# Score steps of two batches moved to stand with the transposes of the step before, and four unused transposes put ahead of a sweep's matmuls

## The chip, the cores and the metric

The kernel runs on one core of one Trainium2 chip, in one launch. The metric is the device time in microseconds (us). Lower is better. The engines' names are those of the profile: PE is TensorE (matmuls and transposes), PEld its weight loads, DVE VectorE, ACT ScalarE, POOL GpSimd, SP the queue that issues the DMAs.

## The reference

Attention over 4 batches, 12 heads, 448 rows and 64 columns a head, with q and k normalised by their root mean square, is followed by a gated layer (768 to 1536 to 768) and a layer with a squared ReLU (768 to 2048 to 768), all in fp32:

```python
q_n, k_n = rmsnorm(q, g_q), rmsnorm(k, g_k)
scores = q_n @ k_n.T / sqrt(64)                 # per batch and head, 448 x 448
attn = exp(scores - max); attn /= attn.sum() + 1e-9
x = (attn @ v)                                  # back to 1792 tokens x 768
x = (sigmoid(x @ w_gate) * (x @ w_val)) @ w_out
h = x @ w_in2
out = (maximum(h, 0) ** 2) @ w_out2             # 1792 x 768
```

## The kernel before

The work is done in four sweeps (`sweep(s)`, L506 to L603), one for each batch of 448 tokens. A sweep takes the attention output of its batch through both layers in 68 blocks of weights: 24 blocks for gate and val, 12 for the first output layer, 16 for the second layer's input, 16 for its output. An fp32 product is split into a high and a low part and made of three matmuls (`mm3`, L495 to L499), each 128 x 128 weights by 448 columns. This text calls those the wide matmuls: L497, L498, L499, 18 a block, 936 in a sweep. The last 16 blocks use matmuls of 384 columns (L596, L597, L598).

While sweep s runs, the attention of batch s+1 is made beside it. `slots_of` (L619 to L760) writes that attention as a list of slots, and the loop at the end (L867 to L884) runs one or two slots after each block. `later(n, ...)` puts a follow-up n blocks on, `mid` puts one into the next block. Batches 2 and 3 (made beside sweeps 1 and 2) use the branch `b > 1`. A pair of heads has e = 0 and 1; each head has its 448 rows in two halves c2 = 0 and 1. The steps of a half, and their letters here:

- S, the score step (`do_s2`): four matmuls of 448 columns with 112 columns of weights (L392) into a PSUM tile `att`; then the maximum on DVE (L399, L402), two exponentials on ACT (L411) and the scaling on DVE (L419 to L422).
- T, the transposes (`do_c2`): eight transposes of that half's exponentials, in two groups of four with 128, 128, 128 and 64 output rows (L431), then copies on ACT (L441, L442) and remainders on DVE (L447, L449).
- V, the product with v (`do_pv2`): seven matmuls of 448 columns (L457, L459), then L463 on ACT and L469 on DVE. After the second head of a pair `x_hi` (L329, ACT) and `x_lo` (L333, DVE) write the pair's rows of the next sweep's input.
- A (`do_a2`): eight transposes of q and k of the next pair (L241), then `a_hi` (L368, L369 on ACT), `a_lo` (L376, L379 on DVE) and `a_dma` (L386), which copies halves of `qs` between partitions.

The pool `att` has two tiles, and S, T, V and A all take one. `qs` has one buffer: the next pair's can be written when the last S of the pair has read the present one. In the slots before, S, T, S, A, V and T of a head stand one after the other, mostly one to a slot. Instructions on one engine run in the order in which the scheduler put them, which takes from the program's order what its own timing holds ready.

Of the kernel before, what the change touches and what calls it, by code (L numbers as in the profile page):

```python
# [17 lines left out]
def attention_moe_moe2_kernel(  # L18
# [14 lines left out]
    nc = tc.nc  # L33
    B, H, S, D = q.shape
# [8 lines left out]
    QR = S // QC  # L43
    NF = S // 128
    TAIL = S - 128 * NF
# [17 lines left out]
    ident = const.tile([128, 128], F32, name="ident")  # L63
# [9 lines left out]
    def att_tile():  # L73
        return att_p.tile([128, 2, 512], F32, tag="att", name="att")
# [281 lines left out]
    def split_v(st):  # L356
        t = st.pop("v")
        vs = one.tile([128, NF + 1, 4, D], F32R, tag="vs", name="vs")
        nc.scalar.copy(out=vs[:, :, 0::3], in_=t)
        nc.vector.tensor_tensor(out=vs[:, :, 1:3], in0=t, in1=vs[:, :, 0::3].bitcast(F32), op=ALU.subtract)  # L360
        st["vs"] = vs
# [26 lines left out]
    def s_mm2(st, e, c2, ps):  # L388
        for i in range(2):
            c = 2 * c2 + i  # L390
            for z in range(2):
                nc.tensor.matmul(  # L392
                    out=ps[:QR, i, :S], lhsT=st["qs"][:, e, z, c * QR:(c + 1) * QR], rhs=st["ks"][:, e],
                    start=(z == 0), stop=(z == 1))
        st["s", e, c2] = ps

    def s_max2(st, e, c2):
        nm = sm_p.tile([QR, 2], F32, tag="nm", name="nm")
        nc.vector.tensor_reduce(out=nm, in_=st["s", e, c2][:QR, :, :S], axis=AX.X, op=ALU.max, negate=True)  # L399
        rq = st["ms"][:, 1].rearrange("p (c h) -> p c h", h=2)[:, 2 * c2:2 * c2 + 2, e]  # L400
        with tc.high_priority(offset=200):
            nc.vector.tensor_tensor(out=nm, in0=nm, in1=rq, op=ALU.mult)  # L402
        st["nm", e, c2] = nm
# [21 lines left out]
    def c_mm2(st, e, c2):  # L425
        ps = att_tile().rearrange("p a (k c) -> p (a k) c", k=2)
        p = st.pop(("p", e, c2))
        for i in range(2):
            for kc in range(NF + 1):
                n = 128 if kc < NF else TAIL  # L430
                nc.tensor.transpose(  # L431
                    ps[:n, kc, i * QR:(i + 1) * QR], p[:, i, kc * 128:kc * 128 + n], ident[:QR, :QR])
        if c2 == 0:
            parts = one.tile([128, NS, S], F32R, tag="pt", name="parts")
            st["ph", e], st["pl", e] = parts[:, 0:NF + 1], parts[:, NF + 1:NS]
        st["c", e, c2] = ps

    def c_hi(st, e, c2):
        ps, ph = st["c", e, c2], st["ph", e]
        cs = slice(c2 * QW, (c2 + 1) * QW)  # L440
        nc.scalar.copy(out=ph[:, 0:NF, cs], in_=ps[:, 0:NF, 0:QW])  # L441
        nc.scalar.copy(out=ph[:TAIL, NF, cs], in_=ps[:TAIL, NF, 0:QW])  # L442
# [9 lines left out]
    def pv_mm2(st, e):  # L452
        o = st["o", e] = att_tile()[:, 0, :S]
        ph, pl = st.pop(("ph", e)), st.pop(("pl", e))
        for kc in range(NF + 1):
            lhsT = st["vs"][:, kc, 2 * e:2 * e + 2].rearrange("p a d -> p (a d)")
            nc.tensor.matmul(out=o, lhsT=lhsT, rhs=ph[:, kc], start=(kc == 0), stop=(kc == NF))  # L457
            if kc < NF:
                nc.tensor.matmul(out=o, lhsT=lhsT, rhs=pl[:, kc], start=False, stop=False)  # L459

    def pv_half(st, e):
        xt = st["xt"] = tmp_p.tile([128, 512], F32, tag="tmp", name="xt")
        nc.scalar.copy(out=xt[e * D:(e + 1) * D, :S], in_=st["o", e][(1 - e) * D:(2 - e) * D])  # L463
# [17 lines left out]
    def later(n, fn, *args):  # L481
        due.setdefault(now[0] + n, []).append((fn, args))
# [18 lines left out]
    def tmp(name):  # L501
        return tmp_p.tile([128, 512], F32, tag="tmp", name=name)[:, :N]
# [3 lines left out]
    def sweep(s):  # L506
        t0 = s * N
        x = xtile[s]
        low = nc.vector
        hb = one.tile([128, 12288], F32R, tag="hr", name="hb")  # L510
        ht = hb[:, 0:2 * K1 * N].rearrange("p (a k n) -> p a k n", a=2, k=K1)
        for m in range(K1):
            for i in range(2):
# [15 lines left out]
                if i == 0:  # L529
                    t = tmp("t")  # L530
                    e = tmp("e")
# [74 lines left out]
    pairs = {}  # L606
# [7 lines left out]
    def nxt(b, hp):  # L614
        return (b, hp + 1) if hp + 1 < HP else (b + 1, 0)
# [3 lines left out]
    def slots_of(b):  # L619
        slots = []  # L620

        def add(*fns):
            slots.append(fns)
# [48 lines left out]
        def do_s2(key, e, c2):  # L672
            st = pairs[key]
            s_mm2(st, e, c2, att_tile())
            s_max2(st, e, c2)
            mid.append((s_exp2, (st, e, c2)))
            later(1, s_norm2, st, e, c2)

        def do_c2(key, e, c2):
            st = pairs[key]  # L680
            c_mm2(st, e, c2)
            c_hi(st, e, c2)
            later(1, c_lo, st, e, c2)

        def do_pv2(key, e):
            st = pairs[key]
            pv_mm2(st, e)
            pv_half(st, e)
            later(1, pv_add, st, e)
            if e == 1:  # L690
                later(2, x_hi, st)
                later(2, x_lo, st)
                later(2, lambda: pairs.pop(key))
# [10 lines left out]
        if b > 1:  # L704
            for h in range(H):
                key, e = (b, h // 2), h % 2
                nk = nxt(*key)
                prev = ((b, (h - 1) // 2), (h - 1) % 2)
                more = nk[0] < B

                def some(fn, nk=nk, more=more):
                    return [lambda: fn(nk)] if more else []

                add(lambda key=key, e=e: do_s2(key, e, 0), *(some(do_load) if e == 0 else []))
                if h:
                    add(lambda prev=prev: do_c2(*prev, 1))
                add(lambda key=key, e=e: do_s2(key, e, 1))
                if e == 1 and more:
                    add(*some(do_a2))
                if h:  # L720
                    add(lambda prev=prev: do_pv2(*prev))
                if e == 0:
                    add(lambda key=key: do_c2(key, 0, 0), lambda key=key: split_v(pairs[key]), *some(do_stat))
                else:
                    add(lambda key=key: do_c2(key, 1, 0), *some(do_v))
            add(lambda: do_c2((b, HP - 1), 1, 1))
            add(lambda: None)
            add(lambda: do_pv2((b, HP - 1), 1))
            return slots
# [5 lines left out]
        for hp in range(HP):  # L735
            key, nk = (b, hp), nxt(b, hp)
            prev = (b, hp - 1)
            more = nk[0] < B
# [176 lines left out]
```

## Time and profile before

| | |
|---|---|
| median of 3 runs | 1321.3 us (1319.93 to 1321.75) |
| the profiled execution | 1321.59 us |
| its span, first to last instruction | 1319.5 us |
| PE busy | 1294.7 us, 98% |
| DVE busy | 923.0 us, 70% |
| ACT busy | 772.0 us, 59% |
| last sweep, wide matmuls | 1055.82 to 1249.25 us |

PE is busy nearly all the time, and "busy" counts a pipelined matmul until its modelled end, 0.36 us after its start, while the next starts 0.20 us after it. What a matmul costs PE in a row is therefore read from start to start, here called a step.

### The profile page before, as it was taken

What the parts mean: (1) busy time and instruction counts of PE and PEld (TensorE: products, weight loads), DVE (VectorE), ACT (ScalarE), POOL (GpSimd) and SP (SyncE); (2) the same over time, 40 slices, a digit from 0 to 9 for tenths busy, and PEclk for the clock granted to TensorE, in tenths of its full rate; (3) what the DMA queues carried; (4) which work ended last, traced back from release to release, by engine and by line L of the source; (5) the groups of instructions that cost most, each with busy time, mean ns of one, the idle gap of its engine ahead of it and who ended that gap; (6) DMA issues with size and microseconds to landing.
All of it is one profiled execution on the core that took longest, in us unless ns stands there. A gap on an engine that the chain in (4) does not pass through costs nothing.

```text
span 1319.5 us, 19162 instructions
## 1 busy us (share of the span) xinstructions
PE 1294.7 (98%) x6920; PEld 1124.8 (85%) x6920; DVE 923.0 (70%) x1544; ACT 772.0 (59%) x1552; POOL 83.9 (6%) x32
## 2 busy tenths in 40 slices
PE   8999999999999999999999999999999999999998
PEld 5554587788797999999999999999999999999998
DVE  6776999889998678768875478777797544435521
ACT  5764677568666667656654477764665455424421
POOL 2200001110110000000000000000000000000000
PEclk8999999999999999999999999999999999999999
DMA  6326987887878444344343534433323343333331
GB/s 152 74 82 209 280 271 244 243 275 225 259 216 279 133 112 120 98 118 112 100 112 107 141 99 110 121 103 114 103 86 111 117 123 108 108 108 106 102 119 46
DMA packets 160158, 189.61 MB, mean 144 GB/s; under 512 B 76096, under 2 KB 119616, under 8 KB 160064
## 3 DMA queue, kind: packets, MB, share of 16 engines
q1 hardware_dynamic: 158208, 187.93, 48.3%
q8 instruction: 55, 0.90, 0.3%
q10 hardware_dynamic: 1856, 0.46, 0.2%
q14 instruction: 39, 0.32, 0.1%
HBM read 150.60 MB, written 32.24 MB: 139 GB/s over the span
## 4 chain that ended last, share of the span: by engine, by line
PE 78%; DVE 8%; DMA 5%; ACT 3%; issue 3%; POOL 1%; SPq 1%; ACTq 0%; DVEq 0%; POOLq 0%
PE acc L497 16%; PE acc L499 16%; PE acc L498 16%; PE acc L596 5%; PE acc L598 5%; PE acc L597 5%; PE att L392 3%; PE att L431 3%; DMA w<-wraw 2%; PE att L259 2%; DMA raw<-in_moe_w_gate_dram 2%; PE att L457 1%; PE acc L307 1%; POOL ms L229 1%; DVE wraw L143 1%
## 5 line engine op out<-in xcount | busy, mean ns | idle before, releaser
L162 DVE TENSOR_TENSOR wsp<-wraw,wsp 128x768 fp32r<-128x768 f32 x260 | 247.9, 954 | 136.4 <-ACT wsp L161 132.7
L497 PE MATMUL acc<-xy,wsp 128*128 128x448 f32 x888 | 329.3, 371 | 2.2 <-ACT rl L573 2.2
L498 PE MATMUL acc<-xy,wsp 128*128 128x448 f32 x888 | 328.0, 369 | 0.0
L499 PE MATMUL acc<-xy,wsp 128*128 128x448 f32 x888 | 327.9, 369 | 0.0
L161 ACT CAST wsp<-wraw 128x768 fp32r<-128x768 f32 x260 | 216.7, 834 | 137.4 <-PE acc L598 65.7
L497 PEld LDWEIGHTS acc<-xy,wsp 128*128 128x128 f32 x888 | 167.7, 189 | 19.7 <-ACT rl L573 2.4
L498 PEld LDWEIGHTS acc<-xy,wsp 128*128 128x128 f32 x888 | 167.8, 189 | 16.6 <-issue 2.2
L499 PEld LDWEIGHTS acc<-xy,wsp 128*128 128x128 f32 x888 | 167.7, 189 | 15.9 <-issue 1.3
L229 POOL TENSOR_TENSOR ms<-ms,mhalf 112x16 f32<-112x16 f32 (+1 forms) x25 | 83.1, 3328 | 894.7 <-DVE ms L228 796.2
L596 PE MATMUL acc<-wsp,rb 128*128 128x384 f32 x384 | 129.2, 337 | 0.0
L598 PE MATMUL acc<-wsp,rb 128*128 128x384 f32 x384 | 129.0, 336 | 0.0
L597 PE MATMUL acc<-wsp,rb 128*128 128x384 f32 x384 | 128.8, 335 | 0.0
L497 PE MATMUL acc<-hb,wsp 128*128 128x448 f32 x288 | 107.3, 373 | 0.0
L498 PE MATMUL acc<-hb,wsp 128*128 128x448 f32 x288 | 106.5, 370 | 0.0
L499 PE MATMUL acc<-hb,wsp 128*128 128x448 f32 x288 | 106.2, 369 | 0.0
L411 ACT ACTIVATE p<-att,nm,ms 112x448 f32<-112x448 f32 x96 | 68.8, 723 | 48.4 <-DVE nm L402 48.4
L134 ACT ACTIVATE wraw<-raw 128x768 f32<-128x768 f32 x56 | 51.4, 917 | 62.0 <-DMA w<-wraw 41.7
L275 ACT ACTIVATE p<-att,nm 112x448 f32<-112x448 f32 x96 | 60.2, 637 | 29.9 <-DVE nm L265 29.7
L573 ACT ACTIVATE rl<-acc 128x448 f32<-128x448 f32 x64 | 34.8, 543 | 70.0 <-PE acc L499 68.6
L598 PEld LDWEIGHTS acc<-wsp,rb 128*128 128x128 f32 x384 | 72.1, 188 | 1.4 <-issue 1.3
L596 PEld LDWEIGHTS acc<-wsp,rb 128*128 128x128 f32 x384 | 72.1, 188 | 1.1 <-issue 0.7
L597 PEld LDWEIGHTS acc<-wsp,rb 128*128 128x128 f32 x384 | 72.1, 188 | 0.1
(125 smaller groups left out, 2091.8 us busy)
## 6 DMA issues: line engine op xcount, KB each, us to landing
wraw<-w SPq DMA_DIRECT2D x204, 384.0 KB, 3.1
w<-wraw SPq DMA_DIRECT2D x56, 384.0 KB, 6.1
raw<-in_moe_w_out_dram SPq DMA_DIRECT2D x28, 768.0 KB, 5.4
raw<-in_moe_w_in_dram SPq DMA_DIRECT2D x16, 768.0 KB, 6.3
raw<-in_moe_w_gate_dram SPq DMA_DIRECT2D x12, 768.0 KB, 6.1
raw<-in_moe_w_val_dram SPq DMA_DIRECT2D x12, 768.0 KB, 5.9
out_dram<-ob SPq DMA_DIRECT2D x28, 192.0 KB, 3.0
qs<-qs SPq DMA_DIRECT2D x24, 224.0 KB, 3.4
```

The lines of the kernel that those rows point to most:

```text
L134: size = nc.scalar.activation(out=t, in_=hi.bitcast(F32), func=AF.Copy, scale=2.0 ** -112)
L161: nc.scalar.copy(out=sp[:, 0], in_=t)
L162: nc.vector.tensor_tensor(out=sp[:, 1], in0=t, in1=sp[:, 0].bitcast(F32), op=ALU.subtract)
L229: nc.gpsimd.tensor_tensor(out=ms, in0=ms, in1=mhalf[:QR, 0:ms.shape[1]], op=ALU.pow)
L275: nc.scalar.activation(out=p[:, e], in_=ps[:QR, e, :S], func=AF.Exp, bias=nm[:, e:e + 1], accum_out=su[:, c, e:e + 1])
L411: nc.scalar.activation(out=p[:, i], in_=ps[:QR, i, :S], func=AF.Exp, bias=nm[:, i:i + 1], scale=rq[:, 2 * c2 + i, e:e + 1], accum_out=su[: ...
L497: nc.tensor.matmul(out=o, lhsT=wh, rhs=xh, start=start, stop=False)
L498: nc.tensor.matmul(out=o, lhsT=wh, rhs=xl, start=False, stop=False)
L499: nc.tensor.matmul(out=o, lhsT=wl, rhs=xh, start=False, stop=stop)
L596: nc.tensor.matmul(out=o, lhsT=rh, rhs=wh, start=(k1 == 0), stop=False)
L597: nc.tensor.matmul(out=o, lhsT=rh, rhs=wl, start=False, stop=False)
L598: nc.tensor.matmul(out=o, lhsT=rl, rhs=wh, start=False, stop=(k1 == K2 - 1))
```

## The change

`sweep` gets four transposes of the identity matrix at the start of the last sweep (s = 3), with the output shapes of one group of T, into a tile that nothing reads. The slots of batches 2 and 3 are written in another order: S of half 0 and T of the head before's half 1 share a slot; A has the next one (an empty slot for e = 0); V the next, with the statistics; S of half 1 and T of half 0 share one; an empty slot ends the head. A stands in the program ahead of the second S of the same pair's second head, where it stood behind it.

```diff
@@ sweep(s)
         hb = one.tile([128, 12288], F32R, tag="hr", name="hb")
+        if s == B - 1:
+            edge = att_tile()
+            for kc in range(NF + 1):
+                n = 128 if kc < NF else TAIL
+                tc.keep_in_program_order(nc.tensor.transpose(
+                    edge[:n, 0, kc * QR:(kc + 1) * QR], ident[:QR, :n], ident[:QR, :QR]))
@@ slots_of(b), b > 1
-                add(lambda key=key, e=e: do_s2(key, e, 0), *(some(do_load) if e == 0 else []))
+                first = [lambda key=key, e=e: do_s2(key, e, 0)]
                 if h:
-                    add(lambda prev=prev: do_c2(*prev, 1))
-                add(lambda key=key, e=e: do_s2(key, e, 1))
-                if e == 1 and more:
-                    add(*some(do_a2))
-                if h:
-                    add(lambda prev=prev: do_pv2(*prev))
+                    first.append(lambda prev=prev: do_c2(*prev, 1))
+                add(*first, *(some(do_load) if e == 0 else []))
+                add(*(some(do_a2) if e == 1 else [lambda: None]))
+                add(*([lambda prev=prev: do_pv2(*prev)] if h else []), *(some(do_stat) if e == 0 else []))
                 if e == 0:
-                    add(lambda key=key: do_c2(key, 0, 0), lambda key=key: split_v(pairs[key]), *some(do_stat))
+                    add(lambda key=key: do_s2(key, 0, 1), lambda key=key: do_c2(key, 0, 0),
+                        lambda key=key: split_v(pairs[key]))
                 else:
-                    add(lambda key=key: do_c2(key, 1, 0), *some(do_v))
+                    add(lambda key=key: do_s2(key, 1, 1), lambda key=key: do_c2(key, 1, 0), *some(do_v))
+                add(lambda: None)
```

Lines behind L510 have numbers higher by 6 in the changed file. The instructions then stand in another order on the engines. First PE, where the last sweep begins, before:

```order
L596 MATMUL acc<-wsp,rb 128x384
L597 MATMUL acc<-wsp,rb 128x384
L598 MATMUL acc<-wsp,rb 128x384
L497 MATMUL acc<-xy_7162,wsp 128x448
L498 MATMUL acc<-xy_7162,wsp 128x448
L499 MATMUL acc<-xy_7162,wsp 128x448
```

and now, 15 wide matmuls further on:

```order
L457 MATMUL att<-parts,vs 128x448
L459 MATMUL att<-parts,vs 128x448
L457 MATMUL att<-parts,vs 128x448
L515 MATMUL att<-ident 128x112 x3
L515 MATMUL att<-ident 64x112
L497 MATMUL acc<-xy_7162,wsp 128x448
L498 MATMUL acc<-xy_7162,wsp 128x448
L499 MATMUL acc<-xy_7162,wsp 128x448
```

The new transposes (L515) stand behind the last V of batch 3, which has moved from 36 matmuls ahead of the sweep's end to behind the 14th wide matmul of the next; 921 of the 936 wide matmuls follow them. Second, PE at the second score step of the first head of the fourth pair of batch 3 (`qs_8474` before, `qs_8458` now is that pair's), before:

```order
L498 MATMUL acc_8602<-hb_7163,wsp_8521 128x448
L499 MATMUL acc_8602<-hb_7163,wsp_8521 128x448
L392 MATMUL att_8672<-ks_8473,qs_8474 112x448 x4
L497 MATMUL acc_8680<-hb_7163,wsp_8562 128x448
L498 MATMUL acc_8680<-hb_7163,wsp_8562 128x448
L499 MATMUL acc_8680<-hb_7163,wsp_8562 128x448
```

and now:

```order
L457 MATMUL att_8696<-parts_8547,vs_8330 128x448
L392 MATMUL att_8741<-ks_8457,qs_8458 112x448 x4
L431 MATMUL att_8749<-ident_90,p_8642 128x112 x3
L431 MATMUL att_8749<-ident_90,p_8642 64x112
L431 MATMUL att_8749<-ident_90,p_8642 128x112 x3
L431 MATMUL att_8749<-ident_90,p_8642 64x112
L497 MATMUL acc_8967<-xy0_8240,wsp_8812 128x448
```

Here S has T directly behind it, and stood among wide matmuls before. Of the 48 score steps of both batches 8 stand so; the others still have between 2 and 90 matmuls before the next transposes. Third, ACT at A of the same pair (`qs_8962` and `qs_8914` are the next pair's), before:

```order
L411 ACTIVATE p_8918,su2_8919<-att_8904,nm_8909,ms_8307 112x448 x2
L573 ACTIVATE rl_8940<-acc_8912 128x448
L161 CAST wsp_8968<-wraw_8822 128x768
L368 CAST ks_8961<-att_8952 64x448
L369 ACTIVATE qs_8962<-att_8952,gqk_92 64x448
L368 CAST ks_8961<-att_8952 64x448
L369 ACTIVATE qs_8962<-att_8952,gqk_92 64x448
```

and now:

```order
L161 CAST wsp_9198<-wraw_9071 128x768
L369 ACTIVATE qs_8914<-att_8904,gqk_92 64x448
L368 CAST ks_8913<-att_8904 64x448
L369 ACTIVATE qs_8914<-att_8904,gqk_92 64x448
L582 ACTIVATE rb_8764<-rl_9189 128x384
L582 ACTIVATE rt_8765<-rl_9189 128x64
L411 ACTIVATE p_9031,su2_9032<-att_9001,nm_9006,ms_8275 112x448 x2
```

The writes of `qs` stood behind the exponentials of the pair's last S, and now stand ahead of them.

## Rows read from the trace of the kernel before

**Rows 1.** The page: span, busy time of each engine
```profile
span 1319.5 us, 19162 instructions
PE 1294.7 (98%) x6920; PEld 1124.8 (85%) x6920; DVE 923.0 (70%) x1544; ACT 772.0 (59%) x1552; POOL 83.9 (6%) x32
```

**Rows 2.** Windows, core 0: busy us (instructions) of PE, PEld, DVE, ACT, POOL; clock, DMA
```profile
437.40:674.20 236.80, 236.80 (x1258) 217.28 (x1257) 184.08 (x347) 156.82 (x324) 14.71 (x5) 1.00 0.39 110
...
756.40:992.00 235.60, 235.60 (x1253) 216.55 (x1252) 184.66 (x346) 156.10 (x324) 14.72 (x5) 1.00 0.37 107
...
1055.80:1249.20 193.40, 193.40 (x938) 175.69 (x937) 92.20 (x139) 89.78 (x164) 0.00 (x0) 1.00 0.36 109
```

**Rows 3.** Timeline of PE, last sweep's wide matmuls: start us, duration us
```profile
1055.82 0.36 PE L497 MATMUL acc<-xy,wsp 128*128 128x448 f32 x1
...
1249.25 0.34 PE L596 MATMUL acc<-wsp,rt 128*128 128x384 f32 x1
```

**Rows 4.** Timeline of PE in sweep 1: a score step, transposes, a score step
```profile
583.16 0.97 PE L392 MATMUL att<-ks,qs 128*112 128x448 f32 x4
...
584.17 0.36 PE L498 MATMUL acc<-hb,wsp 128*128 128x448 f32 x1
...
587.67 0.93 PE L431 MATMUL att<-ident,p 112*128 112x112 f32 x8
...
588.66 0.36 PE L498 MATMUL acc<-hb,wsp 128*128 128x448 f32 x1
...
592.11 0.57 PE L392 MATMUL att<-ks,qs 128*112 128x448 f32 x2
```

**Rows 5.** Timeline of PE, the end of sweep 2's wide part
```profile
975.12 0.37 PE L498 MATMUL acc<-xy,wsp 128*128 128x448 f32 x1
...
979.86 0.93 PE L431 MATMUL att<-ident,p 112*128 112x112 f32 x8
...
980.85 0.36 PE L498 MATMUL acc<-xy,wsp 128*128 128x448 f32 x1
...
985.71 0.97 PE L392 MATMUL att<-ks,qs 128*112 128x448 f32 x4
```

**Rows 6.** Timeline of PE in sweep 0: four transposes among wide matmuls
```profile
321.80 0.55 PE L241 MATMUL att<-ident,qk 112*128 112x112 f32 x4
...
322.40 0.36 PE L497 MATMUL acc<-xy,wsp 128*128 128x448 f32 x1
```

**Rows 7.** Groups of ACT, 880 to 960 us: count, busy us, mean ns
```profile
L463 ACT COPY xt<-att 64x448 f32<-64x448 f32 x3 | 1.6, 528 | 0.9 <-PE att L457 0.9
L329 ACT CAST xy<-x 128x448 fp32r<-128x448 f32 x1 | 0.6, 550 | 0.0
```

**Rows 8.** Line L601, all executions: ns min/median/max, first and last start
```profile
L601 ACT COPY ob<-acc x28: 471/480/504, 403.0 to 1316.0; 128x384 f32<-128x384 f32 x28
```

**Rows 9.** Groups of DVE, 880 to 960 us
```profile
L162 DVE TENSOR_TENSOR wsp<-wraw,wsp 128x768 fp32r<-128x768 f32 x18 | 17.2, 953 | 2.6 <-ACT wsp L161 2.3
L399 DVE TENSOR_REDUCE nm<-att 112x2 f32<-112x896 f32 x6 | 6.5, 1084 | 0.5 <-PE att L392 0.5
L574 DVE TENSOR_TENSOR r<-rl 128x448 f32<-128x448 f32 x8 | 5.0, 621 | 0.9 <-ACT rl L573 0.9
L578 DVE TENSOR_TENSOR rb<-r,rb 128x384 fp32r<-128x384 f32 x7 | 3.9, 553 | 0.2 <-ACT rb L576 0.2
L376 DVE SCALAR_TENSOR_TENSOR qs<-att,gqk,qs 64x448 fp32r<-64x448 f32 x4 | 2.7, 683 | 1.5 <-ACT qs L369 1.4
L469 DVE TENSOR_TENSOR x<-att,xt 64x448 f32<-64x448 f32 x3 | 1.9, 619 | 0.1
```

**Rows 10.** The page's DMA issues: size, median us to landing
```profile
qs<-qs SPq DMA_DIRECT2D x24, 224.0 KB, 3.4
```

**Rows 11.** Timeline of PE, narrow matmuls at the end of sweep 1
```profile
746.00 0.34 PE L596 MATMUL acc<-wsp,rt 128*128 128x384 f32 x1
...
746.87 0.33 PE L598 MATMUL acc<-wsp,rt 128*128 128x384 f32 x1
```

## The prediction

> **What bounds the kernel now.** I read the page first: PE is busy 98% of the span, DVE 70% and ACT 59% [rows 1]. Then the windows by stage: in both sweeps in which batches 2 and 3 are prepared, and in the last sweep's wide part, PE is busy for the whole of each window at a granted clock of 1.00, the 2.4 GHz level [rows 2]. The list of waits, asked for PE from 437.4 us to the end, is empty. From there on nothing but PE's own steps makes the time: the change is worth what it alters in them, plus any wait that it creates.
>
> Last I read the timeline of PE from start to start, and there one matmul has two prices. In the last sweep 936 wide matmuls run from 1055.82 to 1249.25 us [rows 3]: 193.43 / 936 = 0.2067 us a step. In sweep 1, after a score step, 17 steps take from 584.17 to 587.67, 0.206 us each; eight transposes follow, and behind them 17 steps take from 588.66 to 592.11 [rows 4], 0.2029 us. At the end of sweep 2 the same turn is seen: 23 steps from 975.12 to 979.86, 0.206 us, then transposes, then 24 steps from 980.85 to 985.71, 0.2025 us [rows 5]. The two fast stretches make 41 steps in 8.31 us, so I take 0.2027 us for the fast level, 0.2067 us for the slow one, and 0.0040 us for the difference. Clock, shape and line are the same at both, and PE waits at neither.
>
> I followed every stretch of wide matmuls down the timeline. A stretch keeps its level to its end. Behind T (the eight transposes of exponentials) all 32 stretches long enough to tell are fast. Behind A 8 of 10 are fast; behind four transposes in a row (in sweep 0) 8 of 8 are, one of which is in [rows 6]. Behind S 23 of 35 are slow. V leaves the level as it was, 16 of 16. In sweeps 1 and 2 652 of the 1872 wide matmuls stand in slow stretches, and all 936 of the last sweep, which has neither S nor T. It came out of sweep 2's narrow matmuls slow.
>
> The Trainium skill, "TensorE: Matmul & The Clock Gate", section "Back-to-back issue gap", gives the isolated step as the columns over 2.4 GHz plus 2.5 ns, the same for any matmul of the same width; worked out for 448 columns that is an estimate of 0.189 us. The trace stands at neither, 0.2067 and 0.2029 us [rows 3, 4], and differs at equal width, so the measurement decides here; what follows if the rule were right about the one level is the first rival's mechanism.
>
> **The change part by part.**
>
> *Four transposes ahead of the last sweep.* They add four to PE. The like of it, four transposes of 112 columns in sweep 0, starts at 321.80, and the second matmul behind it at 322.40 [rows 6]: 0.60 less one step of 0.20, so 0.40 us. By the order on PE 921 wide matmuls come behind them. If these take the fast level the gain is 921 x 0.0040 = 3.7 us. The new ones have the shapes of one group of T's two, and a group of four behaved in the same way in sweep 0; no row shows exactly these (128, 128, 128, 64 alone, after V). The ends are 0 and 3.7 us; I take 3.7, since all 40 nearest stretches are fast. Part sum: 0.4 - 3.7 = -3.3 us. The 15 matmuls ahead of them may be at either level, 0.06 us.
>
> *V of batch 3's last head moves into the last sweep.* Its seven steps cost PE 7 x 0.20 in either place. What it adds is a chain that was covered by 36 matmuls: on ACT L463, 0.53 us, and `x_hi`, 0.55 [rows 7], with three copies of 0.48 us queued between them [rows 8], while DVE does L469, 0.62 [rows 9]. That is 0.53 + 1.44 + 0.55 = 2.5 us to the high part, and about 0.6 more to the low part. PE meanwhile has the four transposes and 24 wide matmuls, 0.4 + 24 x 0.2027 = 5.3 us, since the order puts the three matmuls that need those rows behind them. Cost nothing; without that cover it would be 2 to 3 us.
>
> *Score steps ahead of transposes.* If each S had T directly behind it, no slow stretch would follow: 652 x 0.0040 = 2.6 us is the most that it can give. But of 48 score steps only 8 stand so. In the wide part 929 matmuls now lie between an S and the next transposes, where 962 did. The reason is `att`. The second S of a pair's second head must run before `a_hi` may overwrite `qs`; A's tile is freed only after `a_lo`; so that head's first T, which takes that tile, comes 35 to 45 matmuls after the S it was written with. Behind A, 227 now follow where 372 did. With the shares seen before (572 of those 962 behind S slow, 80 of 372 behind A) I get 552 + 49 = 601 slow for 652: 50 x 0.0040 = -0.2 us. The shares can turn out otherwise: all fast would be -2.6 us, all of 1156 slow (1156 - 652) x 0.0040 = +2.0 us. I take -0.2, because the counts hardly change; near it, -1 to +1 us is likely.
>
> *The writes of `qs`.* ACT's L369 now waits for the pair's last S, and what is queued behind it (the squares of the layer's activations, L573's and L576's kind, and the exponentials) waits with it; PE needs the result for the next pair's first S, directly behind T. From the end of the last S: DVE has the maximum 1.08, one remainder 0.62, one 0.55, and a weight split 0.95 ahead of L376, 0.68 us [rows 9], then the DMA of `qs` lands 3.4 us on [rows 10]: 7.3 us, and two small instructions besides that I put at 0.2 us each, 7.7. PE has 35 to 45 steps and T, whose price is 588.66 - 587.67 - 0.20 = 0.79 us [rows 4]: 7.9 us where it is shortest (35), 9.9 where it is longest (45), 8.1 where 42 narrow matmuls fill it (five steps from 746.00 to 746.87 [rows 11], 0.174 us each). Hidden, by 0.2 us at the tightest. A pair has one such place, ten in all. Bounds: 0, and below nothing it can't go, as PE does not wait there now; above, the second rival's price. I take 0.
>
> Sum: -3.7 + 0.4 - 0.2 = -3.5 us. The profiled execution took 1321.6 us (span 1319.5 and 2.1 around it), 0.3 over the median of the runs, 1321.3. So 1318.1 against itself and 1317.8 against the median; I say 1317.9 us.
>
> **The rivals.** *The transposes do not set the last sweep's level.* For it: it went in slow out of 16 blocks of narrow matmuls, and sweep 1 began in the same way with 18 slow ones; two of ten stretches after A were slow; a group of four with a short last one was never seen alone. Against it: 40 of 40 after T or a group of four. It would give -0.2 + 0.4: 1321.5 us. The rule of one step for one width would end here too.
>
> *The next pair's first S waits for `qs`.* It takes the place of nothing that PE waits for now. For it: the chain of 7.7 us against 7.9. One more weight split of 0.95 us on DVE ahead of L376, and half a microsecond of other queueing, makes 9.2. By the ten places (9.7, 8.7, 7.9, 9.9, 8.1 and 9.1, 9.3, 7.9, 9.9, 8.1 us of cover) PE then waits 0.5 + 1.3 + 1.1 + 0.1 + 1.3 + 1.1 = 5.4 us: 1317.9 + 5.4 = 1323.3 us. It outweighs the gain from a chain of 8.85 us on. Against it: the same queues before left PE no wait after 437.4 us.
>
> *The score steps do gain what they might.* If the stretches that remain behind S are fast, 2.4 us more: 1315.5 us. For it: the level after S looks set by where S falls, and that is moved everywhere. Against it: S at most 10 steps after T left a slow stretch in 11 of 12 cases, and in ten places S now follows T directly.
>
> **How the numbers follow.** Forecast 0.67, transposes without effect 0.12, the wait 0.13, the larger gain 0.08. The forecast's own range is 1316.8 to 1319.2, from the score steps' -1 to +1 us and 0.2 us of run to run. The range of 8 in 10 takes in the third rival's edge and the first: 1316.0 to 1321.9. What a measurement can tell from no change is about 0.2%, 2.6 us, so faster means under 1318.7. Of the forecast some 0.83 lies below: 0.67 x 0.83 + 0.08 = 0.63 faster. Same: 0.67 x 0.17 + 0.12 and a third of the wait's 0.13 (PE losing 1 to 3 us) = 0.27. Slower: the rest, 0.10.
>
> **What would show it.** Right: the last sweep's 921 wide matmuls take 0.2027 us a step, 186.7 us for 190.4; PE has no wait in the last sweep; the wide parts of sweeps 1 and 2, 236.8 and 235.4 us, stay within 1 us. Wrong: steps of 0.2067 us behind L515; a wait of L392 for the DMA of `qs` or for L376; wide parts of sweeps 1 and 2 shorter or longer by more than 1.5 us; a wait of L497 for `x_hi` at the last sweep's start.

## The result, and the profile after

The changed kernel is slower: 1329.92 us (median of 6 runs, 1326.29 to 1333.33) against 1319.47 (6 runs, 1318.68 to 1321.75) in the same rounds, a ratio of 1.0074, 95% interval 1.0054 to 1.0093. Forecast were 1317.9 us and a range of 1316.0 to 1321.9. The profiled execution took 1326.29 us.

The page of the changed kernel, span and busy time of each engine:

```profile
span 1324.1 us, 19099 instructions
PE 1294.6 (98%) x6924; PEld 1123.9 (85%) x6924; DVE 922.8 (70%) x1544; ACT 772.9 (58%) x1552; POOL 82.2 (6%) x32
```

PE is as busy as before [rows 1], in a span that is 4.6 us longer. So it stands still. The list of PE's waits from 433 us on, which was empty before (line waited for: us in total, times, longest):

```profile
PE acc L497 <- ACT rl L579: 3.3, 4, 1.2
PE att L431 <- DVE x L469: 2.9, 6, 0.6
PE acc L497 <- ACT ob L607: 0.7, 1, 0.7
PE att L459 <- DVE parts L447: 0.7, 1, 0.7
PE acc L602 <- ACT ob L607: 0.3, 1, 0.3
```

The same stages as in [rows 2], from the first wide matmul to the first narrow one:

```profile
433.15:671.33 238.18, 235.59 (x1238) 214.83 (x1237) 174.65 (x324) 152.19 (x311) 15.97 (x5) 1.00 0.38 108
757.17:994.46 237.29, 234.70 (x1233) 214.12 (x1232) 175.21 (x324) 152.73 (x312) 15.60 (x5) 1.00 0.37 106
1060.83:1253.41 192.58, 191.85 (x949) 177.51 (x948) 93.94 (x143) 91.22 (x168) 0.00 (x0) 1.00 0.36 109
```

Before, PE's busy time was the whole of each window; now 2.6, 2.6 and 0.7 us are missing. The narrow parts behind sweeps 1 and 2 are longer by 3.5 and 2.6 us (671.33 to 757.17 and 994.46 to 1060.83, against 674.28 to 756.58 and 992.00 to 1055.82).

**Where T waits.** PE in sweep 1, the last V step, S, T and the first wide matmul:

```profile
610.75 0.37 PE L457 MATMUL att<-parts,vs 128*128 128x448 f32 x1
610.96 0.98 PE L392 MATMUL att<-ks,qs 128*112 128x448 f32 x4
612.40 0.98 PE L431 MATMUL att<-ident,p 112*128 112x112 f32 x8 [0.46 <-DVE x L469]
613.86 0.49 PE L497 MATMUL acc<-xy,wsp 128*128 128x448 f32 x1 [0.48 <-ACT rl L579]
```

ACT and DVE beside it:

```profile
611.15 0.53 ACT L463 COPY xt<-att 64x448 f32<-64x448 f32 x1 [0.54 <-PE att L457]
...
613.27 0.53 ACT L579 ACTIVATE rl<-acc 128x448 f32<-128x448 f32 x1
...
611.71 0.63 DVE L469 TENSOR_TENSOR x<-att,xt 64x448 f32<-64x448 f32 x1
```

V holds one of the two `att` tiles and S takes the other. T needs a third: it starts 0.06 us after L469 has read V's tile. From the last S matmul to the first transpose this takes 0.83 us at its shortest, against a step of 0.20. V, S and T stand in a row in six places, and T waits in all six: from S to T 5.1 us in place of 1.2.

The Trainium skill says in "Perfetto Trace Analysis", section "Optimization Strategy", that a gap which repeats on the engine that should be full can mean too little PSUM for the next tile. The trace agrees: six times the same wait.

**Where the wide matmuls wait.** PE at 630 us (A, then V, then a wide matmul), and ACT:

```profile
630.33 0.93 PE L241 MATMUL att<-ident,qk 112*128 112x112 f32 x8
631.03 0.45 PE L457 MATMUL att<-parts,vs 128*128 128x448 f32 x1
...
632.33 0.37 PE L457 MATMUL att<-parts,vs 128*128 128x448 f32 x1
633.88 0.47 PE L497 MATMUL acc<-xy,wsp 128*128 128x448 f32 x1 [1.19 <-ACT rl L579]
```

```profile
631.30 0.53 ACT L368 CAST ks<-att 64x448 fp32r<-64x448 f32 x1
632.74 0.53 ACT L463 COPY xt<-att 64x448 f32<-64x448 f32 x1 [0.91 <-PE att L457]
633.29 0.54 ACT L579 ACTIVATE rl<-acc 128x448 f32<-128x448 f32 x1
```

L579 frees the `acc` tile that L497 wants. The last wide matmul ahead of A was issued at 630.12 and ended 0.36 us later, so the tile was ready to be read then, but on ACT L579 stands behind the copy of A and the copy of V, and the latter waits 0.91 us for V. PE then does nothing until L579 is done: 1.55 us from V's last matmul to L497, twice in the kernel. A stands directly ahead of V at seven places, and PE waits behind V only at these two, where 12 wide matmuls stand between the last T and A; at the others there are 31 or more.

**The account,** from the first wide matmul of sweep 1 to the last matmul, start to start. Before: 437.52 to 1315.64, 878.1 us. After: 433.15 to 1319.82, 886.7, so 8.55 more.

- Thirteen steps in which PE waits, 12.3 us where thirteen such steps without a wait would take 2.0: +10.3.
- Shorter waits within S, T and V: +1.9.
- The spare transposes: +0.3. Narrow steps: +0.1.
- Wide steps without a wait: -4.1, of which -3.6 in the last sweep.

What came ahead of sweep 1 was 4.4 us shorter in this execution, 433.15 for 437.52. The change doesn't reach there, and a second execution of it (below) had 436.52. So the runs lie some 10 us apart and the two profiles 4.7.

### The profile page after: what moved, and what is told of

Read it like the earlier page. It is cut to its first block, busy times and chain, and to the rows that moved or that the text cites. A ratio compares the mean times of both kernels' runs of the same rounds, so it can differ in the third digit from the quotient of the medians.

```text
span 1324.1 us, 19099 instructions
## 1 busy us (share of the span) xinstructions
PE 1294.6 (98%) x6924; PEld 1123.9 (85%) x6924; DVE 922.8 (70%) x1544; ACT 772.9 (58%) x1552; POOL 82.2 (6%) x32
## 4 chain that ended last, share of the span: by engine, by line
PE 72%; DVE 10%; DMA 7%; ACT 5%; issue 4%; SPq 1%; POOL 1%; ACTq 0%; DVEq 0%; POOLq 0%
PE acc L497 15%; PE acc L498 14%; PE acc L499 14%; PE acc L602 5%; PE acc L604 5%; PE acc L603 5%; DMA w<-wraw 4%; PE att L431 3%; PE att L392 3%; DVE wraw L141 2%; DVE wraw L143 2%; DVE nm L265 2%; PE att L457 1%; PE acc L307 1%; DMA raw<-in_moe_w_gate_dram 1%
## 5 line engine op out<-in xcount | busy, mean ns | idle before, releaser
L497 PE MATMUL acc<-xy,wsp 128*128 128x448 f32 x888 | 327.0, 369 | 5.2 <-ACT rl L579 4.5
L497 PEld LDWEIGHTS acc<-xy,wsp 128*128 128x128 f32 x888 | 166.7, 188 | 23.7 <-ACT rl L579 7.0
L497 PE MATMUL acc<-hb,wsp 128*128 128x448 f32 x288 | 106.4, 371 | 0.0
L399 DVE TENSOR_REDUCE nm<-att 112x2 f32<-112x896 f32 x48 | 52.3, 1090 | 22.4 <-PE att L392 22.0
```

The costliest lines, as they stand in the source:

```text
L497: nc.tensor.matmul(out=o, lhsT=wh, rhs=xh, start=start, stop=False)
```

## The experiments

In the table "distance" is the same stretch as in the account, less the 878.1 us of before; "waits" is the sum of PE's list from sweep 1 on; "last wide" runs from the first wide matmul of the last sweep to the first narrow one (193.4 before). The ratio is to the kernel before, with its 95% interval. The names are those of the sections that follow.

| kernel | distance | waits | last wide | ratio |
|---|---|---|---|---|
| changed | +8.6 | 7.9 | 192.6 | 1.0074 (1.0054 to 1.0093) |
| e1 transposes alone | -3.3 | none | 189.8 | 0.9964 (0.9952 to 0.9976) |
| e2 slots alone | +9.2 | 8.3 | 192.6 | 1.0063 (1.0044 to 1.0083) |
| e3 S and T apart | +12.1 | 7.0 | 196.3 | 1.0081 (1.0063 to 1.0098) |
| e4 A behind S | +7.0 | 5.4 | 196.3 | 1.0039 (1.0024 to 1.0055) |
| e5 V in `acc` | -3.0 | 0.4 | 189.8 | 0.9978 (0.9966 to 0.9991) |
| e6 V's copy on DVE | +11.9 | 10.2 | 195.9 | 1.0082 (1.0065 to 1.0100) |
| e7 one transpose | -3.6 | none | 189.8 | 0.9966 (0.9951 to 0.9982) |
| e8 one behind each S | +14.7 | none | 189.8 | 1.0123 (1.0110 to 1.0136) |
| e9 T of the head before with S | +0.1 | none | 193.4 | 1.0010 (0.9996 to 1.0025) |
| e10 second S behind V | +4.3 | 4.4 | 192.6 | 1.0048 (1.0030 to 1.0066) |
| e11 the same, V ahead of A | +0.8 | 2.7 | 192.6 | 1.0016 (1.0001 to 1.0032) |
| e12 e10 with V in `acc` | +3.3 | 5.0 | 189.8 | 1.0024 (1.0012 to 1.0036) |
| e15 transposes past the wait | +9.2 | 8.3 | 193.0 | 1.0069 (1.0050 to 1.0089) |
| e16 the same on e3 | +8.8 | 7.4 | 193.0 | 1.0075 (1.0056 to 1.0094) |

### The two halves of the change: e1 and e2

e1 is the kernel before with the four transposes, e2 the changed kernel without them.

> The kernel before with only the four spare transposes ahead of the last sweep. Theory A (the transposes set the step of the wide matmuls behind them, and hold it to the end of the sweep): 921 wide matmuls at 0.2027 instead of 0.2067 us, less 3.7, plus 0.4 for the transposes, so about 1316.2 us, 0.2 to 0.3% faster than before. Rival (the gain seen in the last sweep of the changed kernel comes from the order of its slots): those 921 stay at 0.2067 us and the time is 1319.9, within 0.2% of before. Both expect that no wait for L469 or for L579 and L607 appears that before did not have.

> The changed kernel without the four spare transposes. Theory A: the loss is all of the new slots, and the transposes took 3.3 us off it, so about 3 us slower than the changed kernel (1333 where that has 1330), with TensorE's waits of the changed kernel in sweeps 1 and 2 (six of L431 for L469, two of about 1.5 us for L579) at the same places. Rival (the spare transposes bring the loss, by the wait of 0.96 us that stands at the first L497 and what follows it): back to within 2 us of before.

PE in the last sweep of e1:

```profile
1054.86 0.55 PE L515 MATMUL att<-ident 112*128 112x112 f32 x4
1055.18 0.45 PE L497 MATMUL acc<-xy,wsp 128*128 128x448 f32 x1
...
1244.96 0.34 PE L602 MATMUL acc<-wsp,rt 128*128 128x384 f32 x1
```

936 steps in 189.78 us are 0.2028 each, where [rows 3] had 0.2067: -3.65, the longer first step (0.28) included, and +0.32 for the transposes. Theory A holds for e1, and no wait came. For e2 both theories missed. The waits of sweeps 1 and 2 are all there, so the slots make the loss, as theory A has it. But e2 is not slower than the changed kernel: the intervals of 1.0063 and 1.0074 overlap, and its last sweep, without the transposes, ran at the fast level too:

```profile
1062.29:1254.86 192.57, 191.45 (x944) 1.00 0.36 110
```

So the two parts do not add up. In the new order the last sweep is fast without the transposes; more on that in e13 to e16.

### What T and L497 wait for: e3 to e6

e3 gives the second S and the transposes a slot each. e4 moves A. Both start from the changed kernel:

```diff
 e3
+                add(lambda key=key, e=e: do_s2(key, e, 1))
                 if e == 0:
-                    add(lambda key=key: do_s2(key, 0, 1), lambda key=key: do_c2(key, 0, 0), ...)
+                    add(lambda key=key: do_c2(key, 0, 0), ...)
                 else:
-                    add(lambda key=key: do_s2(key, 1, 1), lambda key=key: do_c2(key, 1, 0), *some(do_v))
+                    add(lambda key=key: do_c2(key, 1, 0), *some(do_v))
-                add(lambda: None)
```

```diff
 e4
-                add(*(some(do_a2) if e == 1 else [lambda: None]))
+                if e == 0:
+                    add(lambda: None)
...
                     add(lambda key=key: do_s2(key, 1, 1), lambda key=key: do_c2(key, 1, 0), *some(do_v))
+                    add(*some(do_a2))
                 add(lambda: None)
```

> The changed kernel with the second score step of each head in a slot of its own and the transposes in the next slot, the one that was empty: V, S and T no longer stand in a row. Theory A (T waits for the att tile that V's copies have not freed yet): the six waits of L431 for L469 go, 6 x 0.65 = 3.9 us, and the time is about 4 us under the changed kernel's, 1326; the waits of wide matmuls for L579 stay. Rival (the loss is ACT's order of copies, and the six waits only take the place of waits that would come a few steps later): the six go, the waits of L497 for ACT grow by as much, and the time stays within 1 us of the changed kernel's.

> The changed kernel with the three matmuls of A for the next pair moved from ahead of V to the slot behind the pair's last transposes, the one that was empty. Theory B (ACT works in order, and its copy of A stands ahead of the releases of the wide matmuls' tiles): the waits of 1.5 us at 632.33 and 955.61 us and the two of 0.7 us ahead of them go, 2.7 to 4 us less than the changed kernel. Rival (those waits come of ACT's copy behind V, L463, which stays where it is): they stay, and the time is within 1 us of the changed kernel's. A second rival: the later copy of A makes the next pair's first score step wait for its qs, L392, by up to 2 us a pair, and the time is slower than the changed kernel's.

e3 did not do what it was made for: V, S and T still stand in a row in the same six places of PE's queue, since slots say only from where on a step may be placed. The wait is unchanged:

```profile
PE att L431 <- DVE x L469: 2.9, 6, 0.6
```

It tells nothing for or against theory A there. In e4 the waits moved. V, S and T no longer stand in a row, and L431 waits nowhere; those of L497 for L579 fell to 0.8 us. In their place stand two that the changed kernel lacked or had in small, the second of them the price of A's delay:

```profile
PE att L459 <- DVE parts L447: 1.9, 2, 0.9
PE att L392 <- DMA qs<-qs: 1.6, 1, 1.6
```

So theory B and its second rival were both right in part, and the kernel gained back some 0.35% of 0.74% (1.0039 for 1.0074, intervals that just touch), although its last sweep ran at the slow level.

e5 and e6 leave the slots and change what holds V's tile:

```diff
 e5, in pv_mm2; `wide` is set while the wide matmuls run
-        o = st["o", e] = att_tile()[:, 0, :S]
+        o = st["o", e] = acc_tile()[:, :S] if len(wide) == 1 else att_tile()[:, 0, :S]
 e6, in pv_half
-        nc.scalar.copy(out=xt[...], in_=st["o", e][...])
+        nc.vector.tensor_copy(out=xt[...], in_=st["o", e][...])
```

> The changed kernel, with V's output in an acc tile instead of an att tile while the wide matmuls run (in the narrow parts it stays in att). Theory A (T waits for the att tile that V holds until L463 and L469 have read it): the waits of L431 for L469 in the wide parts, 4 x 0.65 = 2.6 us, are gone, and the time is 2 to 4 us under the changed kernel's. Rival (acc tiles are as scarce): L497 and L457 wait for acc in their place, and the time is within 1 us of the changed kernel's or above it.

> The changed kernel with V's copy L463 on DVE instead of ACT. Theory B (ACT works in order; its copies L463 wait for V, and the Relu and ob copies that free acc tiles stand behind them): the waits of L497 for ACT L579 and L607, 3.1 + 1.4 + 0.8 us in the changed kernel's trace, fall under 1.5 us together, and the time is 3 to 5 us under the changed kernel's; the wait behind the spare transposes is gone and the 921 steps behind them stand at 0.2027. Rival (it is the copy of A, L368, that holds ACT): the waits stay, within 1 us of the changed kernel. A second rival: DVE, which then does both reads of V's tile and waits for V in order, is late for T's reads, L447, and the waits of L431 and L459 grow.

e5 takes the whole loss away: 0.9978 for 1.0074. All that is left of PE's waits:

```profile
PE acc L457 <- ACT parts L441: 0.4, 2, 0.2
```

That is more than theory A asked for, as the waits for L579 went too. PE's order also changed with the tile: in the wide parts V's seven matmuls never stand in one row, but the first, or the first three, some wide matmuls ahead of the rest. So e5 shows that tile and order together made the loss, and can't say how much was either's. Its wide steps without a wait give 5.4 us in the account, where e1's give 3.7; the 1.7 us more stand in sweeps 1 and 2. The steps and waits of S and V cost 2.1 more than before. And of its -3.0 the transposes alone give 3.3 (e1), so the new slots still cost some 0.3 us.

e6 is a miss for theory B as I had put it. With V's copy off ACT the waits went up:

```profile
PE acc L497 <- ACT rl L579: 2.8, 2, 1.4
PE att L431 <- DVE x L469: 2.7, 2, 1.4
PE att L459 <- DVE parts L447: 2.3, 4, 0.7
```

DVE now did both reads of V's tile and was late for T's, as the second rival said. PE no longer waits behind A and V, but at two other places for L579, which stands behind another ACT instruction that waits for V, the one that rewrites `vs`:

```profile
611.75 0.62 ACT L359 CAST vs<-v 128x512 fp32r<-128x512 f32 x1 [0.56 <-PE att L457]
```

So e6 moved one of ACT's waits for V and left others: it shows that this copy alone isn't the cause, not that ACT's order is none. The transposes stand directly ahead of the wide matmuls here, and all but the first five steps behind them are at the fast level, as theory B said. The 195.9 us come from two waits of V ahead of the transposes and a stretch at the 1.2 GHz level behind them.

### Transposes and their price: e7 and e8

```diff
 e7, e8: in sweep(s), in the kernel before
+        if s == B - 1:
+            tc.keep_in_program_order(nc.tensor.transpose(att_tile()[:QR, 0, 0:QR], ident[:QR, :QR], ident[:QR, :QR]))
 e8: also at the end of s_mm2
+        tc.keep_in_program_order(nc.tensor.transpose(
+            ps[:QR, 1, S:512], ident[:512 - S, :QR], ident[:512 - S, :512 - S]))
```

> The kernel before with a single spare transpose ahead of the last sweep instead of four. Theory C (any transpose right ahead of a wide matmul sets the level): 0.03 us for it, the wide steps behind it at 0.2027, so -3.7 us against the kernel before, 0.3 us better than with four. Rival (it takes a row of them, as in T, or it was chance in the one profile): the steps stay at 0.2067 and the time within 0.2% of before.

> The kernel before with a single spare transpose ahead of the last sweep and one behind every score step of batches 2 and 3 (48 of them, 64 columns wide, into the unused columns of the step's own tile). Theory C: behind every one of them the wide steps are at 0.2027, so the 670 slow ones of sweeps 1 and 2 go too (670 x 4 ns = 2.7 us), less 48 x 0.03 to 0.1 us: with -3.7 at the last sweep, 3.7 to 5.0 us faster than before, 1 us better than with the four transposes alone. Rival (one narrow transpose does not set the level): 1.4 to 5 us are added, and the time is that of before or up to 0.3% slower.

One transpose does what four do, for 0.03 us and a first step of 0.28: theory C holds for e7. Both e1 and e7 beat both kernels. e8 is a miss of both theories, slower than either said. PE around its first score step, with the weight load of the spare transpose:

```profile
442.11 0.37 PE L392 MATMUL att<-ks,qs 128*112 128x448 f32 x1
442.41 0.26 PE L395 MATMUL att<-ident 64*112 64x64 f32 x1
442.60 0.47 PE L497 MATMUL acc<-xy,wsp 128*128 128x448 f32 x1
442.91 0.37 PE L498 MATMUL acc<-xy,wsp 128*128 128x448 f32 x1
```

```profile
442.40 0.13 PEld L395 LDWEIGHTS att<-ident 64*112 64x112 f32 x1 [0.33 <-issue]
```

The step into it is 0.30 us for 0.20, its own 0.19, and that of the matmul behind it 0.31 for 0.20. In the account that makes 0.38 us a place: 48 of them 18.3, less the 3.65 of the last sweep, are the 14.7. It was the only transpose here with 64 rows of weights; those of T and of the edge have 112. The weight load stands 0.33 us idle and starts with its matmul, not ahead of it. The Trainium skill, "TensorEngine Tiling (Array Packing)", section "Key Properties", says that a change of tiling mode drains TensorE. No row shows a mode; if 64 rows of weights are such a change, the trace is in line with that, at 0.38 us there and back. Whether the 64 rows or the tile shared with the score step made it was not tried apart: the scores take 448 of the tile's 512 columns, so a transpose of 112 doesn't fit beside them.

### One part of the slots at a time: e9 to e12

All are the kernel before, e9 to e11 without transposes, with its slots of batches 2 and 3 written in another order: S0 and S1 are the score steps, Cp the transposes of the head before, C those of this one.

```diff
-  S0 | Cp | S1 | A | V | C
+  e9:  S0 Cp | - | S1 | A | V | C
+  e10: S0 | Cp | A | V | S1 C | -
+  e11: S0 | Cp | V | A | S1 C | -
+  e12: e10's, with e5's line and e7's transpose
```

> One part of the change alone, without spare transposes: the transposes of the head before stand in one slot with the new head's first score step; the second score step, A and V stay where they were. In this order of TensorE's queue no V, S and T follow each other without a wide matmul between them (in sweep 2 one V and T do). Theory A (the loss is the waits where V, S and T stand in a row): at most one wait, within 0.2% of before, 1318 to 1322. Rival (the transposes of the head before are now later, and what hangs on them, V's copies, late too): waits of V for L447 or of T for L469, 3 us or more, 0.3% slower.

> The other part alone, without spare transposes: the second score step goes behind V into the slot of the transposes, A stands ahead of V as before. In TensorE's queue A and V stand in a row at 4 places and V, S at 10, but V, S and T in a row nowhere. Theory A: the six waits of L431 for L469 (3.9 us) are gone, against 1329 of the slots alone 1325. Theory B (ACT's copies in order): the waits of L497 for L579 stay, 2 x 1.3 us and those ahead of them, so it is still 2 to 5 us slower than before. If the loss were T's wait alone, it would be within 0.2% of before.

> As the kernel with the second score step behind V, but with V's slot ahead of A's: ACT then takes V's copy before A's. Theory B (A's copy, L368, and V's, L463, stand in a row on ACT ahead of L579): V and A still stand in a row at 8 places of TensorE's queue, so the waits of L497 for L579 stay at 1 to 3 us. Rival (only the order A then V hurts, since V's copies then come a queue later): these waits are gone, and the time is 2 to 3 us under that of the kernel with A ahead of V.

> The second score step behind V, V in an acc tile in the wide parts, and one spare transpose ahead of the last sweep. Theory A and B together: no wait of T for V's tile, A and V apart in most places, the last sweep's steps at 0.2027 and score steps directly ahead of transposes at 8 places a sweep that also set the level: 2 to 4 us under the kernel before with the spare transpose alone would be the most, 1313; rival (V's wait for its copies, seen with V in acc, remains): 1316 to 1318, no better than the spare transpose alone.

e9 costs nothing: no wait, 0.1 us. Without the second score step behind V there is thus no loss, but that step alone makes only 4.3 us (e10) of the 9.2 of both parts together (e2). In e10 V, S and T in a row are gone and with them every wait of T, as theory A says. Theory B missed: L497 waits 0.4 us for L573 (L579 above), not 2.6 or more. But V now follows T without a wide matmul between, and waits for T's copies:

```profile
PE att L457 <- ACT parts L441: 1.6, 2, 0.8
PE att L459 <- DVE parts L447: 1.3, 2, 0.7
```

Behind the first of the two places PE also ran at half clock for a while (the window 661 to 667 us; behind the second, as long, it did not):

```profile
661.00:667.00 6.00, 4.53 (x16) 0.72 0.31 114
```

From 663.36 to 667.06 ten steps take 0.37 us each on average, the 1.2 GHz level, where 0.20 would do; the idle times ahead of them were 0.81 and 0.66 us. e11 differs from e10 only by V ahead of A, and most of e10's loss is gone. Its whole list:

```profile
PE acc L497 <- ACT rl L573: 1.6, 4, 0.4
PE acc L497 <- ACT ob L601: 1.1, 1, 1.1
```

What went are V's waits for T's copies, 2.9 us in e10, and the steps at half clock. The waits of L497 for L573 did not go, as e11's rival had it: they are 1.6 us, where e10 has 0.4, though none is longer than 0.4. So the time goes with the rival, and its mechanism doesn't. That A then V hurts by itself is not shown either: in e10's trace A stands directly ahead of V at five places, and PE waits behind none of them. In e12 V waits for T's copies:

```profile
PE acc L457 <- ACT parts L441: 5.0, 6, 1.3
```

So V in another tile is no cure by itself: in e12's order only one score step, 0.8 us, stands between T and V at these six places, too little cover for T's copies. e12 is slower than either theory said.

### The level of the last sweep: e13 to e16

e13 is the changed kernel and e14 e3's, once more, one profile each. e15 (the changed kernel) and e16 (e3's) have the transposes 30 wide matmuls later:

```diff
-        if s == B - 1:
+                if s == B - 1 and m == 0 and i == 1:
...
```

> The changed kernel once more, for the step of the wide matmuls behind the wait of 0.99 us at the first L497 of the last sweep. If the program fixes the level, the 921 stand at 0.2027 again and the wide part of the last sweep takes 192.6 us; if each execution deals it anew, 196.2 us is as likely.

> The kernel with S and T in separate slots once more. If the program fixes the level, the wide part of the last sweep takes 196.25 us again, its steps at 0.2067; if each execution deals it, 192.6 is as likely.

> The changed kernel with the four spare transposes 30 wide matmuls later, past the wait at the begin of the last sweep. The wait stays. The 891 steps behind the transposes stand at 0.2027 whichever level the wait leaves, so the wide part of the last sweep takes 192.6 us, as in the changed kernel's profile. If that kernel's level is fixed by the program, the time is the changed kernel's within 1 us; if its timed runs had the slow level in part, it is 1 to 2 us less.

> The kernel with S and T in separate slots, whose last sweep stood at 0.2067 behind the wait, with the transposes 30 wide matmuls later, past the wait. Theory (the wait behind the transposes undoes what they set): 891 x 4 ns = 3.6 us less than that kernel, 1328.5 against 1332, the wide part of the last sweep 192.7 instead of 196.25. Rival (the level of the last sweep hangs on something else in that order): it stays at 196.2 and 1332.

PE at the begin of the last sweep of the changed kernel: the transposes, then a wait of 0.73 us, 0.99 from start to start, for the first of the `ob` copies of sweep 2, which stand behind V's copy on ACT:

```profile
1065.37 0.55 PE L515 MATMUL att<-ident 112*128 112x112 f32 x4
1066.64 0.47 PE L497 MATMUL acc<-xy,wsp 128*128 128x448 f32 x1 [0.73 <-ACT ob L607]
...
1253.41 0.33 PE L602 MATMUL acc<-wsp,rt 128*128 128x384 f32 x1
```

Behind this wait the changed kernel's 921 steps were fast in both executions and those of e3 slow in both (and e4's). The windows of e13, e14 and e16, one line of each:

```profile
1064.45:1257.02 192.57, 191.84 (x949) 1.00 0.36 109
```

```profile
1061.63:1257.89 196.26, 195.53 (x949) 1.00 0.35 108
```

```profile
1067.38:1260.35 192.97, 191.85 (x948) 1.00 0.35 109
```

In the last sweep two executions of a kernel thus agree to 0.01 us. That does not show that the program fixes the level. In sweep 2 the same 36 wide matmuls, from a wait of L497 to the next S, were fast in the first profile of the changed kernel, 7.41 us, and slow in e13, 7.56:

```profile
937.22 0.47 PE L497 MATMUL acc<-xy,wsp 128*128 128x448 f32 x1 [0.47 <-ACT rl L579]
...
944.63 0.98 PE L392 MATMUL att<-ks,qs 128*112 128x448 f32 x4
```

```profile
940.61 0.49 PE L497 MATMUL acc<-xy,wsp 128*128 128x448 f32 x1 [0.48 <-ACT rl L579]
...
948.17 0.98 PE L392 MATMUL att<-ks,qs 128*112 128x448 f32 x4
```

Of the 65 stretches of nine or more wide matmuls in sweeps 1 and 2, three differ between these two executions, and of e3's 68 seven between e3 and e14; all stand from such a wait on. The kernel before, e1 and e7, in which PE never waits there, agree in all 97.

e16's last sweep is 3.3 us shorter than e3's, the number that its theory gave, but it does not show that the transposes work again past the wait. The 30 steps between the wait and the transposes were fast already, 6.18 us, 0.2024 each without the first of 0.31:

```profile
1073.20 0.47 PE L497 MATMUL acc<-xy,wsp 128*128 128x448 f32 x1 [1.11 <-ACT ob L607]
...
1079.38 0.55 PE L518 MATMUL att<-ident 112*128 112x112 f32 x4
```

e15's are fast as well. The timed runs of e16 against e3 (1330.27 and 1332.00, intervals that overlap) are too close to show a difference. In e2, e10, e11, e15 and e16, without transposes between V and the first L497 behind it, the wait of 1.48 us left the fast level each time; with transposes there, and a wait of 0.99 us, it was fast twice (the changed kernel) and slow three times (e3, e14, e4). So the transposes do not hold the level through a wait, and in the changed kernel they gained nothing over their absence, which is why e2 is no slower. What sets the level behind a wait stays open.

## Why the prediction was wrong

- *Score steps ahead of transposes: -0.2. This is the step that failed.* Of the level it was near: the wide steps of sweeps 1 and 2 took 0.5 us less in the profiled execution and 0.3 less in e13. (Its 652 slow matmuls leave out 18 at the start of sweep 1, and by the traces 359 and 214 stand behind A, not 372 and 227; neither moves the sum.) But the step priced only that. It named where S and T stand, and that `att` sets T's place, and put no wait there. Measured: twelve places with 9.4 us of waits in all, and 1.9 in short ones; the thirteenth is the next item's. T's wait at least could be worked out from the rows shown: from the start of V's last matmul 0.36 us to its end, 0.53 for L463 [rows 7] and 0.62 for L469 [rows 9], 1.51 together, against 1.01 for the five steps that PE has until T. That is 0.5 us a place and 3 us at six, and so nearly the whole gain forecast; measured were 0.65 a place.
- *V of the last head moves into the last sweep: 0.* Too low by 0.96 us. I looked at the consumers of V (`x_hi`, three matmuls), which did not wait. What waited was L497, for `acc` tiles whose copies stand behind V's copy on ACT. The working had listed these three copies between L463 and `x_hi`, and only as a delay to `x_hi`.
- *Four transposes: -3.3.* Right by themselves: e1, -3.65 and +0.32. The changed kernel's account has nearly the same numbers, -3.6 and +0.3, but there that is luck: the transposes stand ahead of a wait, the last sweep is as fast without them (e2), and behind the same wait it was slow in e3 and e4. The two parts of the change do not add: -3.3 (e1) and +9.2 (e2) make 5.9, and measured were 8.6.
- *The writes of `qs`: 0.* Right; L392 never waited. The wait exists in e4, 1.6 us, where A is a slot later.
- *The rivals.* The slower one had the sign and about half the size, 5.4 us, at a place where nothing happened. No rival had `att` or ACT's order. PE was busy 98% of the span and waited nowhere from sweep 1 on, so a new wait for a copy costs in full, and slower should have had far more than 0.10.

What stays open: how the loss divides between tile and order (no kernel changed one alone), and what sets the level behind a wait.

## What to carry to other kernels

When steps that share a small pool of tiles are moved next to each other, count the tiles at each such place, and set the time in which the other engines clear one against what stands between; where nothing does, the difference is the wait. On an engine that works in order, a copy that waits for a late matmul also holds all releases queued behind it, so look for who waits for those, not only for the copy. Gains measured or argued apart are added only if the one does not change the state on which the other rests.

## What the runs showed of the hardware that was not expected

- A single transpose of 112 rows ahead of 936 wide matmuls took 0.0039 us from each of them (e7), for 0.03 us and a first step longer by 0.08. Where PE never waits, a stretch of wide matmuls had the same level in three executions (97 of 97 in the kernel before, e1 and e7, which have the same order there); behind a wait of 0.47 us it differed between two executions of one kernel.
- A transpose with 64 rows of weights cost 0.38 us between matmuls of 128 rows, and did not always set the level: behind S and such a transpose 13 of 39 stretches were slow (e8), where by the same count the kernel before has 23 of 39 behind S alone.
- After waits of 0.81 and 0.66 us in a row PE ran ten steps at the 1.2 GHz level (e10), 1.7 us more than at the other, and again behind an equal pair in e6 (granted 0.54 from 1068.5 to 1072 us); after an equal pair in e10's next sweep, and after single waits of up to 1.2 us in the changed kernel, it did not.
